# Block-sparse attention with a maxout MLP on one core: v spread by engine copies instead of DMA, maxima of k by a tree, masks and w2-w1 on Pool

## The chip, the core and the metric

The kernel runs on one core of a Trainium2 chip. The engines are TensorE (PE in the profile; PEld is its weight load), VectorE (DVE), ScalarE (ACT), Pool (POOL, GpSimd) and SyncE (SP, which here issues the DMAs). The metric is the time of one execution on the device in microseconds. Every kernel was run several times, beside runs of the kernel before on the same chip. A run is called slow when it is over 1.5% above the fastest of the same kernel; ratios use fast runs alone. A ratio is the mean time of one kernel's fast runs over that of the other's fast runs of the same rounds, so it is not quite the ratio of the medians that are quoted.

## The reference, cut to what matters

```python
# q, k, v: 4 batches, 8 heads, 768 positions, 64 wide
k_sum = k.reshape(B, H, 24, 32, D).max(axis=3)      # one key per block of 32: the maximum
v_sum = v.reshape(B, H, 24, 32, D).mean(axis=3)     # one value per block: the mean
scores_l = scale * q @ k.T, kept where |i - j| < 16 # a band
scores_s = scale * q @ k_sum.T + log(32)            # all 24 blocks
a = softmax over both; attn = a @ [v, v_sum]
x = attn as 3072 x 512
out = maximum(x @ w1, x @ w2) @ w_out               # d_ff 1024
```

The kernels compute the last line as x·(w1·w_out) + relu(x·(w2-w1))·w_out, so that w2-w1 is made once. TensorE does the same matmul work before and after the change (only the block means of v of the first batch come in two halves). (PSUM below is where the kernels place the tiles called `banks`, which their matmuls write; SBUF is where they place all other tiles.)

## The kernel before

Queries go in tiles of 64. A tile's keys are 64 positions on partitions 0 to 63, the 24 block sums on 64 to 95, and 32 positions on 96 to 127. Odd tiles need other partitions of v than even ones, so v has to move across partitions. After the first batch this is done by five DMAs per batch, and a sixth spreads the block means:

```python
for piece, (lo, hi, tiles_, part, ms) in enumerate((
        (0, 64, slice(0, NT, 2), 0, slice(0, NM)),
        (0, 64, slice(1, NT, 2), 64, slice(0, NM)),
        (96, 128, slice(0, NT, 2), 64, slice(0, NM)),
        (96, 128, slice(1, NT - 1, 2), 0, slice(1, NM)),
        (96, 128, slice(NT - 1, NT), 0, slice(0, 1)))):
    # vx[b][lo:hi, tiles_] <- vb[part:part + hi - lo, ms], by DMA
# ... means by TensorE, one copy on VectorE, one DMA "vx<-vx" to the other tiles
```

Per pair of heads, VectorE prepares k with four instructions (`prep`), and it masks the exponentials of the second to fourth batch:

```python
op("DVE", 0.96, ... tensor_copy(out=kt()[:, :, 0:64], in_=order(kps)))        # place k, from PSUM
op("DVE", 0.95, ... tensor_reduce(out=ks, in_=kt() by blocks of 32, op=max))   # 768 -> 24
op("DVE", 0.17, ... tensor_copy(out=kx[:, 96 * NT:KW], in_=kx[:, 0:32]))       # wrap
op("DVE", 0.22, ... tensor_copy(out=kt()[:, :, 64:88], in_=ks repeated))       # sums to all tiles
# scores on TensorE, exp on ScalarE, then
op(mask_on, ..., tensor_tensor(out=pv(), in0=pv(), in1=mask, op=mult))         # mask_on = "DVE"
```

The order of instructions on each engine is fixed when the kernel is built. A small scheduler in the kernel (`Plan`) takes the microseconds that stand in each `op(...)` and a lag per engine ("SP": 2.0 from a load's end to its use), and issues everything in that order. At run time an engine whose next input is late waits, even if inputs of later work are there: in the profiled run before, TensorE stood for 1.75 us, until 70.42, before values products that needed v's spread (L460), while inputs of matmuls ordered behind them were written (`g` of L581 by 64.97; they began at 70.89).

The softmax here doesn't subtract the row's maximum and nothing guards it: scores larger than these inputs give would overflow.

## Time and profile before

Median 193.4 us (192.1 to 195.2). First the page's line of busy times and, from its second part, three rows of 40 slices of 4.8 us (busy tenths) and the clock granted to TensorE:

```profile
PE 166.4 (86%) x1643; PEld 117.9 (61%) x1664; DVE 109.9 (57%) x289; ACT 114.1 (59%) x173; POOL 25.7 (13%) x39
...
PE   0629619899999969999979999999999999999990
DVE  6908956888979438759868953079777600000000
PEclk9999996999999999999999999999999999999999
```

From the ninth slice on (38 us) TensorE shows 9 everywhere but in two slices and the last; most of the holes are before that. The groups of VectorE instructions that the change touches (line, engine, operation, output and inputs, shapes, count | busy us in all, mean ns of one | idle before):

```profile
L375 DVE TENSOR_REDUCE ks<-kx 128x24 bf16<-128x768 bf16 x16 | 15.1, 944 | 0.1
...
L435 DVE TENSOR_TENSOR pb<-pb,mask 128x512 bf16<-128x512 bf16 x24 | 11.0, 464 | 3.1 <-ACT pb L426 3.1
...
L441 DVE TENSOR_TENSOR pb<-pb,mask 128x256 bf16<-128x256 bf16 x24 | 7.9, 369 | 1.7 <-ACT pb L426 1.7
...
L506 DVE TENSOR_TENSOR wd<-wf,wf 128x1024 bf16<-128x1024 f32 x4 | 4.9, 1222 | 0.8 <-DMA wf<-in_moe_w_dram 0.8
...
L382 DVE COPY kx<-ks 128x288 bf16<-128x288 bf16 x16 | 3.7, 229 | 0.0
L379 DVE COPY kx<-kx 128x32 bf16<-128x32 bf16 x16 | 3.4, 215 | 0.0
```

Masks take 18.9 us of VectorE and w2-w1 takes 4.9; the preparation of a pair of heads (placing 955, then 944, 215 and 229 ns) takes 2.34 us.

Four pieces of the chain that ended last (start us, us, what) show what the change is after:

```profile
14.21 8.25 DMA vx<-vb
...
63.29 7.09 DMA vx<-vx
...
70.42 0.63 PE banks L460 x15
...
82.35 10.64 DMA vx<-vb
```

The chain runs three times through DMAs that spread v (first, second and third batch), and at 70.4 us TensorE's values products (L460) start again when the second batch's spread has landed.

Last, busy time by stage (window, its length, then each engine's busy us with its instruction count, granted clock, DMA share, GB/s). The first window is the first batch with the weights, the next two are the rest of the attention mixed with the MLP:

```profile
0.00:46.00 46.00, 29.32 (x322) 22.43 (x324) 33.03 (x85) 24.87 (x33) 16.30 (x31) 0.96 1.04 296
46.00:101.00 55.00, 51.12 (x532) 36.05 (x540) 41.22 (x102) 38.15 (x59) 6.26 (x6) 1.00 1.09 269
101.00:165.00 64.00, 63.13 (x660) 45.93 (x666) 35.67 (x104) 41.93 (x67) 3.17 (x2) 1.00 0.43 113
```

**An account of lost time.** A busy TensorE is not a fast one here (166.4 us busy, where 159.1 would do by the rates that follow), so one more reading is used throughout. In the chain, back-to-back matmuls take 0.056 us (128x128), 0.030 (128x65), 0.109 (128x256) and 0.216 (128x512). With these rates all matmuls of either kernel need 159.1 us. The loss up to a matmul is its end less the work ordered in front of it; time that TensorE spends at half its clock (3.4 us in the first batch of this run) counts as loss too. For the profiled run before, 24.1 us are lost until the last values product of the first batch, 2.7 more until that of the second, 2.1 until that of the third, none after, and 4.5 us are the tail of the last copy and store.

### The profile page before, as it was taken

To read this page: it belongs to the slowest core of one execution; us is meant where nothing else is said; L and a number is where in the kernel's file an instruction comes from. 1 tells how busy PE (TensorE), PEld (TensorE's weight loads), DVE (VectorE), ACT (ScalarE), POOL (GpSimd) and SP (SyncE) were. 2 spreads that over 40 slices of the span, in tenths; PEclk is the share of its full clock that TensorE was granted. 3 is DMA by queue.
4 is the path that set the end of the run, shared out by engine and by line. 5 is a ranking of instruction groups with operands and counts; after the bars stand their busy time and mean duration, and the time that the engine had idled before them with its cause. 6 is when DMAs were issued, how large, how long until landed. Compare 5 with 4: busy or idle time off the path is not lost.

```text
span 192.5 us, 4148 instructions
## 1 busy us (share of the span) xinstructions
PE 166.4 (86%) x1643; PEld 117.9 (61%) x1664; DVE 109.9 (57%) x289; ACT 114.1 (59%) x173; POOL 25.7 (13%) x39
## 2 busy tenths in 40 slices
PE   0629619899999969999979999999999999999990
PEld 0426419865757738758657767487696676665740
DVE  6908956888979438759868953079777600000000
ACT  2533964384689949219967955179986443342621
POOL 7556221300330003300003300000000000000000
PEclk9999996999999999999999999999999999999999
DMA  5999999999999999999999996061020111120303
GB/s 187 226 305 356 234 240 347 371 381 281 210 359 251 292 268 217 339 309 217 229 288 223 340 218 193 3 164 24 3 109 5 54 58 59 50 109 0 112 0 109
DMA packets 47859, 37.27 MB, mean 194 GB/s; under 512 B 26208, under 2 KB 43744, under 8 KB 47840
## 3 DMA queue, kind: packets, MB, share of 16 engines
q1 hardware_dynamic: 47840, 37.01, 71.8%
q8 instruction: 13, 0.21, 0.5%
q14 instruction: 6, 0.05, 0.1%
HBM read 25.17 MB, written 6.29 MB: 163 GB/s over the span
## 4 chain that ended last, share of the span: by engine, by line
PE 53%; DMA 33%; SPq 5%; DVE 4%; POOL 2%; issue 1%; ACT 0%; ACTq 0%
PE banks L581 17%; PE banks L560 16%; DMA vf<-in_v_dram 13%; DMA vx<-vb 10%; PE banks L574 7%; PE banks L460 5%; DMA wf<-in_moe_w_out_dram 4%; SPq L503 4%; DMA vx<-vx 4%; PE banks L414 3%; DMA kqf<-in_k_dram 2%; PE banks L359 2%; POOL vb L340 2%; PE banks L484 2%; PE banks L313 1%; DVE pb L435 1%
## 5 line engine op out<-in xcount | busy, mean ns | idle before, releaser
L560 PE MATMUL banks<-xt,wd 128*128 128x256 bf16 x384 | 46.6, 273 | 0.5 <-DVE xt L489 0.5
L581 PE MATMUL banks<-wo,g 128*128 128x512 bf16 x184 | 44.9, 379 | 0.4
L560 PEld LDWEIGHTS <-wd 128*128 128x128 bf16 x384 | 36.4, 98 | 6.1 <-issue 0.7
L426 ACT ACTIVATE pb<-banks,bias 128x512 bf16<-128x512 f32 x48 | 31.5, 686 | 10.2 <-PE banks L414 9.9
L565 ACT ACTIVATE g<-banks 128x512 bf16<-128x512 f32 x48 | 28.3, 596 | 13.7 <-PE banks L560 13.2
L340 ACT COPY o<-banks 128x512 f32<-128x512 f32 x24 | 14.0, 585 | 28.7 <-PE banks L581 28.4
L388 ACT COPY qx<-banks 64x768 bf16<-64x768 bf16 x32 | 25.3, 791 | 6.1 <-PE banks L359 5.8
L581 PEld LDWEIGHTS <-g 128*128 128x128 bf16 x192 | 17.2, 97 | 16.5
L460 PE MATMUL banks<-vx,pb 128*128 128x65 bf16 x384 | 19.4, 196 | 3.6 <-DMA vx<-vx 1.8
L574 PE MATMUL banks<-w1o,xt 128*128 128x512 bf16 x85 | 21.9, 379 | 0.6
L460 PEld LDWEIGHTS <-pb 128*128 128x128 bf16 x384 | 16.9, 100 | 7.1 <-DMA vx<-vx 2.1
L359 PE MATMUL banks<-identity,kqb 128*128 128x128 bf16 x192 | 16.6, 234 | 5.3 <-DVE kqb L340 4.7
L340 ACT CAST kqb<-kqf 128x768 bf16<-128x768 f32 x16 | 13.1, 830 | 13.6 <-DMA kqf<-in_q_dram 8.7
L414 PE MATMUL banks<-qx,kx 128*128 128x128 bf16 (+2 forms) x208 | 18.6, 226 | 2.3 <-ACT qx L388 1.3
L340 POOL CAST vb<-vf 128x1536 bf16<-128x1536 f32 x8 | 12.2, 1520 | 55.0 <-DMA vf<-in_v_dram 35.2
L474 DVE TENSOR_TENSOR xs<-banks,inv 128x256 bf16<-128x256 f32 x48 | 19.1, 415 | 0.3
L414 PEld LDWEIGHTS <-kx 128*128 128x128 bf16 x208 | 15.1, 103 | 6.6 <-DVE kx L382 2.4
L359 PEld LDWEIGHTS <-kqb 128*128 128x128 bf16 x192 | 13.6, 106 | 8.5 <-DVE kqb L340 4.7
L373 DVE COPY kx<-banks 128x768 bf16<-128x768 bf16 x16 | 15.2, 955 | 2.9 <-PE banks L359 1.7
L375 DVE TENSOR_REDUCE ks<-kx 128x24 bf16<-128x768 bf16 x16 | 15.1, 944 | 0.1
L489 DVE COPY xt<-banks 128x512 bf16<-128x512 bf16 x24 | 9.8, 418 | 7.2 <-PE banks L484 6.8
L574 PEld LDWEIGHTS <-xt 128*128 128x128 bf16 x96 | 8.9, 98 | 7.9
(47 smaller groups left out, 129.8 us busy)
## 6 DMA issues: line engine op xcount, KB each, us to landing
kqf<-in_k_dram SPq DMA_DIRECT2D x16, 384.0 KB, 6.6
kqf<-in_q_dram SPq DMA_DIRECT2D x16, 384.0 KB, 5.7
vf<-in_v_dram SPq DMA_DIRECT2D x8, 768.0 KB, 10.7
out_dram<-o SPq DMA_DIRECT2D x20, 256.0 KB, 2.2
wf<-in_moe_w_dram SPq DMA_DIRECT2D x8, 512.0 KB, 11.1
vx<-vb SPq DMA_DIRECT2D x6, 396.0 KB, 8.0
wf<-in_moe_w_out_dram SPq DMA_DIRECT2D x4, 512.0 KB, 8.6
vx<-vx SPq DMA_DIRECT2D x4, 363.0 KB, 6.2
```

The lines of the kernel that those rows point to most:

```text
L340: {"DVE": nc.vector.tensor_copy, "ACT": nc.scalar.copy, "POOL": nc.gpsimd.tensor_copy}[engine](out=o, in_=i)
L359: nc.tensor.transpose(out=bank(ps, S, BF16)[:, 128 * j:128 * j + 128], in_=src.ap[:, j].rearrange("p h d -> p (h d)"), identity=identity[:])
L373: op("DVE", 0.96, lambda: nc.vector.tensor_copy(out=kt()[:, :, 0:64], in_=order(kps)), read=[kps], write=[kx[b, hp], kmain], prio=prio, la ...
L388: op("ACT", 0.8, lambda a=a, r=r: nc.scalar.copy(out=qx[b, hp].ap[r, a, :], in_=order(qps)[r]), read=[qps], write=[qx[b, hp]], prio=prio, ...
L414: nc.tensor.matmul(out=o[:, :, n0:n1], lhsT=w, rhs=qx[b, hp].ap[:, :, c:c + n1 - n0], start=(mask_on != "PE"), stop=(mask_on != "PE" or (i ...
L426: op("ACT", 0.7, lambda: nc.scalar.activation(out=pv(), in_=bank(ps).rearrange("p (i w q) -> p i w q", w=2, q=64), func=ACT.Exp, bias=bias ...
L460: nc.tensor.matmul(out=av()[:, u, a, :], lhsT=pb.ap[:, 2 * u + a, 64 * par:64 * par + 128], rhs=vx[b].ap[:, 4 * grp + 2 * u + par, 2 * hp ...
L474: op("DVE", 0.42, lambda: nc.vector.tensor_tensor(out=x.ap[:, hp % 2], in0=av()[:, :, :, 0:D], in1=inv.ap[:].to_broadcast([128, 2, 2, D]), ...
L560: nc.tensor.matmul(out=bank(ps)[:, 256 * s:256 * s + 256], lhsT=wd[n].ap[:, c, 128 * s:128 * s + 128], rhs=x.ap[:, c, :], start=(c == 0), ...
L565: op("ACT", 0.6, lambda n=n, ps=ps: nc.scalar.activation(out=g.ap[:, 2 * n:2 * n + 2, :].rearrange("p f n -> p (f n)"), in_=bank(ps), func ...
L574: nc.tensor.matmul(out=bank(ps), lhsT=x.ap[:, c, sl], rhs=w1o[c].ap[:], start=(c == 0), stop=False)
L581: nc.tensor.matmul(out=bank(ps), lhsT=g.ap[:, f, sl], rhs=wo[f // 2].ap[:, f % 2, :], start=False, stop=(f == FC - 1))
```

## The change

The intent is to get the spread of v off the DMA queues. Even tiles keep their order of keys and odd tiles get another one, so that most of v is already on the right partitions, and the rest moves by VectorE copies within its engine. To make room on VectorE, the maxima are taken by halving (a tree), and the masks and w2-w1 go to Pool. The core of the diff:

```diff
-        op("DVE", 0.95, lambda: nc.vector.tensor_reduce(... 768 -> 24 ...))
-        op("DVE", 0.17, ... wrap k)
-        op("DVE", 0.22, ... sums k, all 12 tiles)
+        op("DVE", 0.28, lambda: ... tensor_tensor(out=fold(16), in0=e[:, :, 0:16], in1=e[:, :, 16:32], op=ALU.max))
+        op("DVE", 0.18, lambda: ... tensor_tensor(... 16 -> 8, op=ALU.max))
+        op("DVE", 0.27, lambda: nc.vector.tensor_reduce(... 192 -> 24 ...))
+        for us, at, n, to, frm in ((0.2, 64, 64, ...), (0.14, 0, 32, ...), (0.1, 0, 32, ...)):
+            op("DVE", us, ... tensor_copy(out=kx[:, 1, to, at:at + n], in_=kx[:, 0, frm, at:at + n]))   # odd k
+        for e, at in ((0, 96), (1, 32)):
+            op("DVE", 0.2, ... sums k, 6 tiles each)
...
-            pbs[hp, grp] = scores(b, hp, grp, p + 5 + grp, "DVE")
+            pbs[hp, grp] = scores(b, hp, grp, p + 5 + grp, "POOL")          # masks, batches 2 to 4
...
-        load_w12(n, (30, 50, 150, 170)[n], 400)
+        load_w12(n, (30, 50, 150, 170)[n], 400, "POOL", "ACT")              # w2-w1, w1 cast
...
-        # v: two casts, five DMA pieces, one DMA of the means
+        # v: cast straight into the even tiles; per batch three copies to the odd tiles,
+        # two copies of the sums from PSUM, two copies that repeat them in five more key tiles, all on VectorE
```

Also w1 is cast on ScalarE instead of Pool, six zeroings go to ScalarE, and v of the first batch is loaded and handled in two halves and cast on VectorE. The exponential loses its bias (the factor 32 of the block sums is now carried by v's extra column), v has one load buffer for eight heads instead of two for four each, and w1's transposes get a buffer of their own.

## The prediction

> **What bounds the kernel now.** TensorE. The page has it busy 166.4 of 192.5 us; in the chain of waits, back to back, 8 matmuls of 128x512 take 1.73 us and 8 of 128x256 take 0.87 us, and with such rates all its matmuls need about 159 us (my sum). The other 33 us are a slow start, holes and a 4.5 us tail. The first values product runs at 29.8 us, behind the v spread by DMA (landed 29.0; the windows show TensorE busy only 14.2 of the first 30 us). By 43.4 us about 20 us of matmul work are done. From there to the last matmul (188 us) only some 6 us are lost, 1.75 of them at 68.5 us on the second batch's spread. DMA is saturated to about 125 us, but after 35 us TensorE fills in with maxout work, so most of that is hidden.
>
> **Removed, added, moved.**
> - DMA: all spreads (5.5 MB; near 27 us of the 16 engines' time). Loads come earlier: w_out starts landing near 35 us instead of 38.9, v of the second batch is complete near 48 instead of 54.1.
> - VectorE per batch: masks go (11.0+7.9 us over three batches, 6.3 each); w2-w1 goes once (4.9). Added: v copies, sums and their spread, about 5 us (from 64x3168 in 0.98 us alone, 32x512 in 0.69). Key preparation stays level: the 0.94 us reduction becomes about 0.75, the 0.4 us wrap and sums 0.85.
> - Pool: 36 masks at an estimated 1.1 us, w2-w1 4 x 2.1, v casts in one piece of 3 us. Busy rises from 26 to about 70 us.
> - ScalarE: zeroing and w1 casts (4 x 1.05), early.
> - TensorE work stays.
>
> **On the critical path.** The v chain of the first batch becomes VectorE work in order: summed from 4.1 us on, I reach the first values at about 28 us, with 1.8 us more matmul work done than before. VectorE then paces that batch to 42 to 44 us. Gain 2 to 3 us. The second batch's values can stall: v landed 48, cast 51, then VectorE copies behind key work, ready about 60 to 62, while TensorE's order wants them near 58. Later batches have over 10 us of slack.
>
> [...] mask products under a Pool cast took 1.22, 1.40 and 1.64 us instead of 0.28 and 0.41; a 0.16 us copy took 1.03. About half of the Pool cast time became VectorE waiting; with some 16 us of Pool reads per batch I expect 6 to 8 us more VectorE time per batch, giving back 4 to 7 us in TensorE stalls. [...]
>
> **Prediction.** 189.8 us, 8 in 10 between 184 and 196. Faster by over 2%: 0.42; within 2%: 0.47; slower by over 2%: 0.11.
>
> **Right or wrong shows in:** first values product near 28 us; no DMA in the chain after 40 us; TensorE gaps after 43 us released by VectorE or Pool, 4 to 7 us; short VectorE copies taking 0.5 to 1.5 us under Pool masks; matmul work unchanged.
>
> **What would make it wrong.** [...] Pool masks so late that values stall each batch (then above 196)[...].

One term of the sum: 184 us, for the case that VectorE hardly waits for Pool. With the 4 to 7 us of stalls on top the sum is 188 to 191 us. The masks' 1.1 us and the 2.1 us of w2-w1 on Pool were no measurements but the durations that the changed kernel gives its scheduler; 3 us for a cast of v is twice the 1.52 us that the half-size casts took before. For "saturated to about 125 us" the trace has a DMA share of 1.04 to 1.14 in every 10 us from 10 to 110 us, 0.91 to 120 us and 0.30 to 130 us.

## The result, and the profile after

The changed kernel takes 201.6 us (201.4 to 201.9, four runs) against 193.4 us: ratio 1.044, 95% interval 1.039 to 1.049. It is slower by 4.4%; 189.8 us with a range to 196 had been predicted. The page's busy times and slices (5.0 us each):

```profile
PE 171.1 (86%) x1670; PEld 120.3 (60%) x1670; DVE 130.3 (65%) x338; ACT 116.5 (58%) x183; POOL 76.8 (38%) x89
...
PE   0579554999996998999978699998899999999991
DVE  6579999886799889759999964059979251000000
PEclk9999996699999999999999999999999999999999
```

VectorE did not get lighter; it went from 109.9 to 130.3 us. After 50 us TensorE had two slices below 9 (a 6 and a 7) in the kernel before; now it has seven (two 6s, a 7 and four 8s), the last slice left out. The groups that answer to those of before:

```profile
L446 POOL TENSOR_TENSOR pb<-pb,mask 128x512 bf16<-128x512 bf16 x24 | 30.8, 1299 | 55.5 <-ACT pb L437 55.2
...
L452 POOL TENSOR_TENSOR pb<-pb,mask 128x256 bf16<-128x256 bf16 x24 | 17.7, 758 | 0.2 <-ACT pb L437 0.2
...
L393 DVE COPY kx<-ks 128x192 bf16<-128x192 bf16 x32 | 11.6, 405 | 0.1
...
L324 DVE COPY vx<-vx 32x2560 bf16<-32x2560 bf16 x6 | 8.9, 1479 | 0.2
...
L374 DVE TENSOR_TENSOR half<-kx 128x384 bf16<-128x384 bf16 x16 | 7.2, 449 | 0.2
...
L382 DVE TENSOR_REDUCE ks<-half 128x24 bf16<-128x192 bf16 x16 | 5.4, 340 | 0.0
L389 DVE COPY kx<-kx 128x384 bf16<-128x384 bf16 x16 | 5.1, 316 | 0.0
L378 DVE TENSOR_TENSOR half<-half 128x192 bf16<-128x192 bf16 x16 | 5.0, 315 | 0.0
L389 DVE COPY kx<-kx 128x160 bf16<-128x160 bf16 x16 | 4.4, 274 | 0.0
```

A pair of heads now costs VectorE 0.95 for placing, 0.45 + 0.32 + 0.34 for the tree, 0.32 + 0.27 + 0.19 for odd k and 2 x 0.41 for the sums, together 3.65 us instead of 2.34. Times 16 pairs that is 21 us, as much as VectorE's whole rise. The masks, w2-w1 and the rest that left it were eaten by the v copies.

A mean of 405 ns hides two kinds of instruction: half of the 32 took 202 ns or less, one took 2811. This is the stretch of the timeline where that one stands (start, us, engine, line):

```profile
74.77 1.29 POOL L452 TENSOR_TENSOR pb<-pb,mask 128x256 bf16<-128x256 bf16 x2
75.02 1.08 DVE L389 COPY kx<-kx 128x160 bf16<-128x160 bf16 x2
76.01 2.75 POOL L334 CAST vx<-vf 128x3072 bf16<-128x3072 f32 x1
76.01 2.81 DVE L393 COPY kx<-ks 128x192 bf16<-128x192 bf16 x1
```

The copy, which takes 0.20 us at the median, ends 0.06 us after Pool's cast, begun at the same moment: by these times it waited for the whole of it. The profile counts all 2.81 us as busy time of VectorE, not as waiting. A second one, at 98.39 us, took 1.16 us and ended 0.07 us after a mask product that Pool had begun 0.28 us before it. By the trace of this run three kinds of VectorE instruction can stretch beside Pool instructions that read: copies between SBUF tiles (up to 2.81 us), casts between them (that of k 1.28 us, 0.55 at the median) and products of two SBUF tiles (384 wide 1.21 us, 0.35 at the median). They are called exposed below. Reductions do not stretch (192 to 24: 0.32 to 0.34 us the four times that a reading Pool instruction ran beside them, 0.32 to 0.35 otherwise), nor does placing k from PSUM (0.94 to 0.96 us, both beside one, seven times, and without).

Busy time by stage, in the windows of before:

```profile
46.00:101.00 55.00, 51.47 (x495) 33.49 (x491) 46.46 (x104) 32.56 (x53) 27.99 (x21) 1.00 0.73 211
101.00:165.00 64.00, 58.84 (x658) 42.94 (x655) 44.95 (x124) 39.36 (x65) 28.18 (x31) 1.00 0.18 61
```

The DMA share falls from 0.43 to 0.18 in the last window, as intended, but VectorE rises by 5 and 9 us and Pool by 22 and 25. In the chain there is no DMA of v any more after the first batch; instead it runs through VectorE for 20 us on end (88.8 to 109.5 us, in the third batch) before TensorE comes next in it, with the transposes of the MLP's input (L495). An excerpt:

```profile
91.66 1.49 DVE vx L324
93.17 1.49 DVE vx L324
94.68 0.36 DVE half L374
...
98.39 0.71 DVE kx L393
...
100.16 1.14 DVE vx L334
...
109.48 0.29 PE banks L495 x2
```

And TensorE waits for VectorE (what waited, for whom, us in total, times, longest). The same two waits in the kernel before, then in the changed one:

```profile
PE banks L414 <- DVE kx L382: 1.0, 1, 1.0
PE banks L460 <- DMA vx<-vx: 1.8, 1, 1.8
...
PE banks L425 <- DVE kx L393: 4.3, 5, 1.6
PE banks L471 <- DVE vx L324: 3.5, 4, 1.5
```

L425 (before L414) are the scores, which need the k sums; L471 (before L460) are the values. In the account of lost time: 25.2 us until the end of the first batch's values (before 24.1), then 4.0, 5.2 and 2.0 for the other three batches (before 2.7, 2.1 and 0), tail 4.2 (4.5). So 6.4 of the 7.2 us between the two profiled runs (199.7 against 192.5) lie after the first batch.

### The profile page after: what moved, and what is told of

The parts are those of the page before. It is cut to its first block, busy times and chain, and to the rows that moved or that the text cites. A ratio compares the mean times of both kernels' runs of the same rounds, so it can differ in the third digit from the quotient of the medians.

```text
span 199.7 us, 4301 instructions
## 1 busy us (share of the span) xinstructions
PE 171.1 (86%) x1670; PEld 120.3 (60%) x1670; DVE 130.3 (65%) x338; ACT 116.5 (58%) x183; POOL 76.8 (38%) x89
## 4 chain that ended last, share of the span: by engine, by line
PE 52%; DVE 21%; issue 4%; POOL 3%; ACT 1%; DVEq 0%; ACTq 0%
PE banks L571 15%; PE banks L592 15%; PE banks L585 7%; DVE vx L324 4%; PE banks L471 4%; PE banks L555 3%; DVE kx L368 3%; PE banks L425 2%; DVE kx L393 2%; POOL pb L446 2%; DVE vx L334 2%; PE banks L495 2%; DVE vx L318 2%; PE banks L312 1%; DVE xs L485 1%
## 5 line engine op out<-in xcount | busy, mean ns | idle before, releaser
L446 POOL TENSOR_TENSOR pb<-pb,mask 128x512 bf16<-128x512 bf16 x24 | 30.8, 1299 | 55.5 <-ACT pb L437 55.2
L592 PE MATMUL banks<-wo,g 128*128 128x512 bf16 x192 | 46.5, 379 | 0.0
L437 ACT ACTIVATE pb<-banks 128x512 bf16<-128x512 f32 x48 | 27.2, 597 | 17.4 <-PE banks L425 15.2
L334 ACT COPY o<-banks 128x512 f32<-128x512 f32 x24 | 14.0, 585 | 32.5 <-PE banks L592 32.3
L399 ACT COPY qx<-banks 64x768 bf16<-64x768 bf16 x32 | 25.3, 791 | 4.8 <-PE banks L353 4.5
L471 PE MATMUL banks<-vx,pb 128*128 128x65 bf16 x384 | 20.6, 197 | 4.8 <-DVE vx L324 3.5
L425 PE MATMUL banks<-qx,kx 128*128 128x128 bf16 (+2 forms) x208 | 18.7, 224 | 6.5 <-DVE kx L393 4.3
L353 PE MATMUL banks<-identity,kqb 128*128 128x128 bf16 x192 | 17.7, 242 | 6.9 <-DVE kqb L334 4.8
L585 PE MATMUL banks<-w1o,xt 128*128 128x512 bf16 x96 | 23.2, 379 | 0.0
L471 PEld LDWEIGHTS <-pb 128*128 128x128 bf16 x384 | 17.7, 100 | 8.9 <-issue 4.8
L425 PEld LDWEIGHTS <-kx 128*128 128x128 bf16 x208 | 15.0, 102 | 11.4 <-DVE kx L393 7.2
L452 POOL TENSOR_TENSOR pb<-pb,mask 128x256 bf16<-128x256 bf16 x24 | 17.7, 758 | 0.2 <-ACT pb L437 0.2
L334 DVE COPY vx<-vx 64x3072 bf16<-64x3072 bf16 (+5 forms) x15 | 15.0, 1017 | 0.3
L483 DVE RECIPROCAL inv<-banks 128x4 f32<-128x4 f32 x48 | 8.0, 173 | 10.2 <-PE banks L471 10.1
```

The costliest lines, as they stand in the source:

```text
L334: {"DVE": nc.vector.tensor_copy, "ACT": nc.scalar.copy, "POOL": nc.gpsimd.tensor_copy}[engine](out=o, in_=i)
L353: nc.tensor.transpose(out=bank(ps, S, BF16)[:, 128 * j:128 * j + 128], in_=src.ap[:, j].rearrange("p h d -> p (h d)"), identity=identity[:])
L399: op("ACT", 0.8, lambda a=a, r=r: nc.scalar.copy(out=qx[b, hp].ap[r, a, :], in_=order(qps)[r]), read=[qps], write=[qx[b, hp]], prio=prio, ...
L425: nc.tensor.matmul(out=o[:, :, n0:n1], lhsT=w, rhs=qx[b, hp].ap[:, :, c:c + n1 - n0], start=(mask_on != "PE"), stop=(mask_on != "PE" or (i ...
L437: op("ACT", 0.6, lambda: nc.scalar.activation(out=pv(), in_=bank(ps).rearrange("p (i w q) -> p i w q", w=2, q=64), func=ACT.Exp, scale=scale),
L446: eng.tensor_tensor(out=pv(), in0=pv(), in1=m, op=ALU.mult)
```

## Experiments

Three theories were put against each other. A: Pool's masks and w2-w1 make VectorE wait, and the change gives VectorE many short exposed instructions. B: VectorE simply has more work, and chains get longer, contention aside. C: the fixed order of instructions was made with too short durations.

In this table "lost" is the account above in us for the profiled run, up to the end of the first batch's values, then the sum over the other three batches; the ratio is to the kernel before in the same rounds. The profiled runs of b_masks_pool and b_wd_pool were slow ones, so their "lost" is not used. The last column is the time at half clock that the trace of the profiled run records in these two stretches; half of it is the most that it can have added to "lost" (an estimate from the distance of back-to-back matmuls: in the profiled run before 0.107 us at half clock instead of 0.056 for 128x128, 0.055 instead of 0.029 for 128x65).

| kernel | ratio (95% interval) | median us | lost in batch 1 | lost in batches 2-4 | half clock, us |
|---|---|---|---|---|---|
| before | 1 | 193.4 | 24.1 | 4.8 | 3.4 / 0 |
| changed kernel | 1.044 (1.039-1.049) | 201.6 | 25.2 | 11.2 | 6.8 / 0 |
| x_masks_fill | 1.007 (0.997-1.018) | 194.9 | 25.2 | 4.7 | 6.8 / 0 |
| x_wd_fill | 1.042 (1.030-1.054) | 201.4 | 25.3 | 11.1 | 13.7 / 0 |
| x_both_fill | 1.006 (0.992-1.020) | 194.1 | 23.9 | 4.4 | 10.2 / 0 |
| x_spread_small | 1.025 (1.012-1.037) | 197.7 | 25.8 | 6.7 | 6.8 / 0 |
| x_masks_dve | 1.008 (1.001-1.015) | 195.3 | 27.7 | 1.9 | 10.2 / 0 |
| x_one_reduce | 1.041 (1.031-1.051) | 202.3 | 27.6 | 9.8 | 13.7 / 0 |
| x_true_times | 1.024 (1.016-1.032) | 200.4 | 24.6 | 9.1 | 6.8 / 3.4 |
| v_masks_times_lag | 1.011 (1.005-1.017) | 197.4 | 30.4 | 2.6 | 17.1 / 0 |
| v_masks_wd_times_lag | 0.998 (0.994-1.002) | 194.5 | 25.5 | 3.4 | 6.8 / 0 |
| b_masks_pool | 0.988 (0.978-0.998) | 192.6 | | |  |
| b_masks_pool_2 | 1.002 (0.996-1.009) | 193.3 | 23.1 | 4.6 | 3.4 / 0 |
| b_wd_pool | 1.001 (0.992-1.010) | 194.3 | | |  |
| b_masks_pool_lag | 1.008 (1.004-1.013) | 196.8 | 25.1 | 6.4 | 6.8 / 0 |
| b_copies | 1.006 (0.997-1.015) | 195.5 | 25.3 | 3.9 | 3.4 / 0 |
| b_masks_pool_copies | 1.030 (1.021-1.038) | 199.9 | 23.7 | 11.3 | 3.4 / 6.8 |
| b_masks_pool_reduce | 1.007 (1.002-1.013) | 194.0 | 23.8 | 6.2 | 6.8 / 3.4 |

Medians are over all runs of a kernel, slow ones too, and the chips differ: the fast runs of the kernel before had means between 192.8 and 194.8 us. The ratios are the figures to compare. The changed kernel itself was timed in the first call only. In the four fills (x_masks_fill to x_spread_small) only two of seven runs of the kernel before count as fast (192.9 and 193.3; the others took 195.8 to 198.3), so those four ratios hang on two runs. Within the call no such run is needed: the fast runs of x_wd_fill, which behaves like the changed kernel, average 201.2 us, those of x_spread_small 197.8, of x_masks_fill 194.5 and of x_both_fill 194.2.

### x_masks_fill: Pool just as busy, but without reading

```diff
-                eng.tensor_tensor(out=pv(), in0=pv(), in1=m, op=ALU.mult)
+                for _ in range(2):
+                    eng.memset(pv(), 1.0)
```

The half-size masks get the same edit. The order on every engine is that of the changed kernel. Its output is wrong, which doesn't matter for the time.

> Wrong result on purpose. The changed kernel with the same order on every engine; each of the 36 mask products on Pool is replaced by memsets of the same tile that take about as long (1.0 to 1.2 us) but read nothing. Theory A [...]: the short VectorE copies under Pool masks go back to 0.2 to 0.35 us, VectorE busy falls from 130 to about 118 us, and the time falls by 3 to 5 us, from 201.6 to 197 to 198.5. Rival B (VectorE simply has more work and longer dependency chains, contention aside): less than 1 us.

```profile
PE 168.2 (87%) x1651; PEld 119.2 (62%) x1670; DVE 121.9 (63%) x338; ACT 116.4 (60%) x183; POOL 73.8 (38%) x137
...
L393 DVE COPY kx<-ks x32: 191/203/1304, 7.7 to 147.8; 128x192 bf16<-128x192 bf16 x32
```

(The second line is of the view of one tile: shortest, median and longest of the 32 sums copies in ns. In the changed kernel they are 173, 202 and 2811.) The ratio falls from 1.044 to 1.007, more than expected, and the loss in batches 2 to 4 falls from 11.2 to 4.7 us, with first-batch loss unchanged at 25.2. VectorE's busy time falls to 121.9 us without one instruction less, and the longest sums copy takes 1.3 instead of 2.8 us. As Pool is about as busy as before (73.8 against 76.8 us) and the clock is alike (0.979 and 0.981 in the profiled runs), it is the reading and not Pool's lateness that costs. Theory A holds for most of the time that was lost. The cut is not even complete: copies are still held up, though less, beside Pool instructions that only write (three that take 1.3 us took 3.00 beside them in the next experiment).

### x_wd_fill and x_both_fill: the same for w2-w1, and both

```diff
-            out=wd[n].ap[:], in0=fs[1].ap[:], in1=fs[0].ap[:], op=ALU.subtract)
+            # a product of 2 columns (keeps the wait for the loads), then
+            nc.gpsimd.memset(wd[n].ap[:], 0.01); nc.gpsimd.memset(wd[n].ap[:], 0.01)
+            nc.gpsimd.memset(wd[n].ap[:, 0:2], 0.01)
```

> Wrong result on purpose. The changed kernel in the same order; each w2-w1 on Pool becomes memsets of about 2.4 us behind a product of two columns (which keeps the wait for the load). Theory A: the odd copies of v of the first batch go from 1.9 and 2.7 us to about 0.55 each, the first values product starts near 27 us instead of 30.2, the time falls by 1 to 3 us. Rival B: under 0.5 us, as VectorE's own work sets that start.

> Wrong result on purpose. Both of the edits before: masks and w2-w1 on Pool read nothing, same order. Theory A: the sum of both, 5 to 7 us less, near 195 us; what then remains over the kernel before (193.4) is VectorE's extra work. Rival B: under 1.5 us.

Alone, the edit changes nothing (1.042): a miss for theory A as I had put it. But the test did not remove the contention. The three odd copies of v of the first batch's second half, which the changed kernel's timeline has at 4.77 us together, still took 3.00 us under the memsets; the first half's three took 1.3 us undisturbed. Besides, TensorE got half its clock from 22.3 to 29.1 and from 32.5 to 39.3 us in this profile, and in the changed kernel's only from 31.6 to 38.4. (The 30.2 us of the expectation is the start of the second half's values in the changed kernel; the first 16 values products start at 27.5.) Both edits together are no better than the masks alone (1.006 against 1.007). What w2-w1 on Pool costs is not settled by these two.

### x_spread_small: less VectorE work, Pool untouched

```diff
-                    out=rs(lo, lo + 32, slice(1, NM)),
+                    out=rs(lo, lo + 32, slice(1, NM))[:, :, :, 0:D if b < 2 else 2],      # and the input alike
```

Same order, wrong result. The two copies of 1.48 us per batch that repeat the block sums nearly vanish in the third and fourth batch.

> Wrong result on purpose. The changed kernel in the same order; in the third and fourth batch the spread of the block sums of v over the key tiles (two copies of 32x2560, 1.48 us each) copies 2 of 64 columns. Theory A: at most 0.7 us faster, since these copies are not slowed by Pool. Rival B (VectorE's added work itself stalls TensorE): 2 to 4 us faster, the gaps near 103 and 140 us shrink.

The ratio falls to 1.025, and the loss of the third batch from 5.2 to 2.7 us, of the fourth from 2.0 to 0.1. So theory B holds too: work alone, of instructions that Pool did not slow (in the changed kernel all six took 1.475 to 1.484 us, and no Pool instruction ran beside any of them), stood on the chain. These copies repeat their input; copies of the same 32x2560 that do not took 0.815 us at the shortest.

### x_masks_dve: masks back on VectorE

```diff
-                pbs[hp, grp] = scores(b, hp, grp, p + 5 + grp, "POOL")
+                pbs[hp, grp] = scores(b, hp, grp, p + 5 + grp, "DVE")
```

> The changed kernel with the masks back on VectorE (the scheduler orders anew); correct result. Theory A [...]: VectorE takes 17 to 19 us of masks back but waits 12 us less, the time falls to 195 to 198 us. Theory B (VectorE's amount of work): VectorE busy near 137 us and the time stays at 200 us or more. If both hold, between: 197 to 200.

Ratio 1.008, correct result. VectorE's busy time hardly moves (132.7 against 130.3 us), although the masks take 15.8 us there (18.9 in the kernel before, where some waited for Pool's casts, up to 1.64 us instead of 0.42). So the rest of VectorE's work takes 13.4 us less. The loss in batches 2 to 4 is 1.9 us, the smallest of all. VectorE does the masks itself in little more time than it lost to Pool's doing them.

### x_one_reduce: the tree undone

```diff
-        # 384-wide maximum, 192-wide maximum, reduction of 192
+        op("DVE", 0.28, lambda: nc.vector.tensor_reduce(out=ks.ap[:, 0:nb], in_=even() by blocks, op=ALU.max))
+        # the two other entries stay in the plan and issue nothing, so that the order stays
```

> The changed kernel in the same order with the two halving maxima and the short reduction made one reduction of 768 again (0.94 us, no second input). Correct result. If the tree saves nothing even undisturbed (its parts take 0.35 + 0.25 + 0.34 us when Pool is idle) and only adds two instructions that wait for Pool: 1 to 2 us faster than 201.6. If the tree is a gain: 1 to 2 us slower.

No difference that the timing can show (1.041 against 1.044, and 1.031 to 1.051 is 2 us to either side), so the expected 1 to 2 us were neither found nor excluded. In the account batches 2 to 4 lose 1.4 us less than in the changed kernel and the first 2.4 more, with twice the time at half clock there. What can be said is that no gain of the tree shows. Undisturbed its parts take 0.35 + 0.25 + 0.34 = 0.94 us, the single reduction takes 0.944. That fits a fixed part of each instruction of 0.14 to 0.15 us, an estimate from two sizes of a kind, if the rest goes with the size: products of 384 and 192 take 0.35 and 0.25 us, reductions of 768 and 192 take 0.944 and 0.34 (the shortest copies here, of 32 elements, took 0.158 at the median). Three instructions pay it three times.

### x_true_times: the order made with the durations of the trace

```diff
-        op("DVE", 0.28 ... 0.18 ... 0.27            # tree
+        op("DVE", 0.35 ... 0.25 ... 0.34
-        "POOL": (1.1, 1.2)                          # masks; odd copies, sums and w2-w1 likewise
+        "POOL": (1.2, 1.4)
```

> The changed kernel, its scheduler given the durations that the trace shows undisturbed (maxima 0.35, 0.25, 0.34 us instead of 0.28, 0.18, 0.27; odd copies 0.25, 0.20, 0.16 instead of 0.20, 0.14, 0.10; spread of the sums 1.48 instead of 0.75; masks on Pool 1.2 and 1.4 instead of 1.1 and 1.2; w2-w1 2.4 instead of 2.1). Rival C (the static order, made with too short durations, costs the time): 4 us or more faster, to 197.5 or less. Theories A and B (the waits and the work cost it whatever the order): at most 2 us faster.

Ratio 1.024, against 1.044: two points, which are 3.9 us of 193.4. That is more than the 2 us that A and B allowed and just short of theory C's 4 us; the interval (1.016 to 1.032) does not decide between them. In the profiled runs the loss falls by 2.7 us in all, although this one has 3.4 us more at half clock. Theory C has a share, as large as that of less spreading. The single effects add up to more than the whole: masks without reads (3.7 points), less spreading (2.0) and better times (2.0) against 4.4. My reading, which no run shows by itself, is that all three cure the same thing: VectorE being later than the order of TensorE assumes.

### b_masks_pool, b_wd_pool: one part of the change alone, on the kernel before

```diff
-                pbs[hp, grp] = scores(b, hp, grp, p + 5 + grp, "DVE")
+                pbs[hp, grp] = scores(b, hp, grp, p + 5 + grp, "POOL")
```

```diff
-        op("DVE", 1.2, lambda: nc.vector.tensor_tensor(out=wd[n].ap[:], ...
+        op("POOL", 2.35, lambda: nc.gpsimd.tensor_tensor(out=wd[n].ap[:], ...
```

> The kernel before with this part of the change alone: masks of the second to fourth batch on Pool. Theory A: VectorE gets rid of 19 us of work, [...] 1 to 5 us slower than before. Theory B: VectorE has less work, so no slower and up to 2 us faster.

> The kernel before with w2-w1 on Pool alone. VectorE is rid of 4.9 us between 25 and 39 us, where after 30 us it paces the first batch[...]. Expected 0.5 to 2 us faster; if the start is set by the spread by DMA alone, within 0.5 us.

Masks on Pool do no harm to the kernel before (0.988 from two fast runs, then 1.002 in the repeat below), which contradicts theory A as expected here (1 to 5 us slower). w2-w1 on Pool changes nothing (1.001). So the same move costs the changed kernel 3.6 points (1.044 against 1.008) and the kernel before nothing. The theory needs another part: what else is on VectorE.

### b_masks_pool_2, b_copies, b_masks_pool_copies, b_masks_pool_reduce: which VectorE work makes masks on Pool dear

To the kernel before, per pair of heads of the second to fourth batch, either five short copies of the shapes of the changed kernel's odd copies and sums are added, or one reduction. Both write a spare tile that nobody reads, and stand on the way to the scores in the scheduler.

```diff
+            op("DVE", us, lambda m=m, n=n: nc.vector.tensor_copy(
+                out=spare[:, 0:m, 0:n], in_=kt()[:, 0:m, 0:n]), read=[kmain], write=[kx[b, hp]], ...)
```

```diff
+        op("DVE", 0.95, lambda: nc.vector.tensor_reduce(
+            out=spare[:, 0, 0:24] ..., in_=kt()[:, :, 0:64] by blocks, axis=AX.X, op=ALU.max), ...)
```

> A repeat of b_masks_pool on the chip of the three that follow. Was 1.2 percent faster than before; expected 0 to 1.5 percent faster.

> The kernel before, masks on VectorE, with five short extra copies per pair of heads in the second to fourth batch (about 1.0 us undisturbed, of the shapes of the changed kernel's odd copies and sums; they write a spare tile, and the result stays right). Pool only casts v here. Exposure: at most 1 percent slower than before. Load: 1 to 2 percent slower, as VectorE gets 12 us more work without the masks leaving it.

> The same extra copies with the masks on Pool. VectorE's work without waits is 7 us below that of b_copies. Exposure: the 60 copies meet masks and stretch by 6 us or more in all; 1.5 to 3 percent slower than b_masks_pool_2 and slower than b_copies. Load: no slower than b_copies.

> Masks on Pool and, instead of the copies, one extra reduction of 768 (0.94 us, not stretched under Pool in any trace so far). Exposure: within 1 percent of b_masks_pool_2 and clearly faster than b_masks_pool_copies. Load: as slow as b_masks_pool_copies, within 0.5 percent.

The added copies with masks on VectorE (b_copies), from the groups by shape:

```profile
L270 DVE COPY spare<-kx 128x192 bf16<-128x192 bf16 x24 | 4.8, 202 | 0.5
L270 DVE COPY spare<-kx 128x384 bf16<-128x384 bf16 x12 | 3.0, 250 | 0.0
L270 DVE COPY spare<-kx 128x160 bf16<-128x160 bf16 x12 | 2.4, 202 | 0.2
L270 DVE COPY spare<-kx 128x32 bf16<-128x32 bf16 x12 | 2.0, 169 | 0.2
```

The same copies with masks on Pool (b_masks_pool_copies):

```profile
L270 DVE COPY spare<-kx 128x192 bf16<-128x192 bf16 x24 | 9.9, 412 | 0.7
L270 DVE COPY spare<-kx 128x160 bf16<-128x160 bf16 x12 | 6.2, 517 | 0.3
L270 DVE COPY spare<-kx 128x384 bf16<-128x384 bf16 x12 | 5.3, 440 | 0.0
L270 DVE COPY spare<-kx 128x32 bf16<-128x32 bf16 x12 | 3.8, 316 | 0.4
```

And the added reduction with masks on Pool (b_masks_pool_reduce):

```profile
L269 DVE TENSOR_REDUCE spare<-kx 128x24 bf16<-128x768 bf16 x12 | 11.3, 939 | 0.0
```

The same 60 copies take 12.2 us in one kernel and 25.2 in the other. The reduction keeps its 0.94 us. Accordingly the copies cost 2.8 points with masks on Pool (1.030 against 1.002) and 0.6 with masks on VectorE, and the reduction costs 0.5. VectorE is equally busy in b_copies and b_masks_pool_copies (119.2 and 119.0 us), yet 1.006 and 1.030 are far apart, so the sum of VectorE's time does not decide. Part of that distance is clock: the runs of b_masks_pool_copies took 197.1 and 197.9 us at a mean clock of 0.99 and 199.9 at 0.974, and of b_copies the two at 0.96 and 0.97 (196.4, 196.6) count as slow and are left out. At equal clock the two kernels are 1.7% apart, and b_masks_pool_copies is 2.6 to 3.1% behind b_masks_pool_2. This answers the question: masks on Pool and short copies on VectorE are cheap alone and dear together, a reduction is not, and the change adds masks on Pool and short copies at once. That it matters that the copies stand on the way to the scores is argued; no run moved them elsewhere.

### v_masks_times_lag, v_masks_wd_times_lag, b_masks_pool_lag: looking for a better version

```diff
-    LAG = {"PE": 0.25, "ACT": 0.2, "DVE": 0.15, "POOL": 0.2, "SP": 2.0}
+    LAG = {"PE": 0.25, "ACT": 0.2, "DVE": 0.15, "POOL": 0.2, "SP": 3.5}
+    # v_...: masks on VectorE and the durations of x_true_times; v_masks_wd_...: w2-w1 on VectorE too
```

> The changed kernel with masks on VectorE, the durations of x_true_times, and 3.5 instead of 2.0 us from a load's end to its use in the scheduler (the trace shows the first loads landing 1.5 to 2 us later than planned, and TensorE waiting 2 us in order for the first w1 cast). TensorE's loss from the end of the first batch's values on was 2 us with masks on VectorE against 5 before; if the first part loses no more than before's 24 us: 190 to 192, faster than the kernel before by 1 to 2 percent. If the first part stays at 26 to 28 us: 193 to 196.

> As v_masks_times_lag with w2-w1 on VectorE too: nothing that reads runs on Pool while the first batch's v is copied. If the odd copies' waits under w2-w1 (4.8 us for three copies that take 1.3 undisturbed) set the first part, 1 to 2 us faster than v_masks_times_lag; if VectorE's sum of work sets it, 1 to 3 us slower.

> The kernel before with masks on Pool and the same 3.5 us for loads in the scheduler. b_masks_pool was 1.2 percent faster than before with an interval that nearly touches zero; if that is real, this too is 0.5 to 2 percent faster than before; if it was chance, within 0.5 percent.

With masks and w2-w1 on VectorE, the longer durations and the later lag, the changed kernel equals the one before (0.998): in this arrangement spreading v by VectorE copies and by DMA come out the same. The pair of v kernels differ only in w2-w1 and the order that follows, and the one with w2-w1 on Pool is 1.3 points slower and loses 30.4 instead of 25.5 us in the first batch; but its profile also has half clock for 17.1 instead of 6.8 us there, which alone may make up to 5.1 us (an estimate: half of the difference), and the orders differ. So the share of w2-w1 stays open. The later lag made b_masks_pool no better (1.008). No version was faster than the kernel before by 2%.

## Why the prediction was wrong

VectorE's waiting for Pool was named, and what it would cost came out at the upper end: masks that read nothing give back 3.7 points, about 7 us, where 4 to 7 were predicted. **The step that failed is the gain that was set against it.** The record had 184 us for the case that VectorE hardly waits for Pool, 9 us below the kernel before; its text accounts for 2 to 3 of them, and after the first batch only 4.8 us were lost. The runs show no such gain: with masks that read nothing the ratio is 1.007, with w2-w1 that reads nothing as well 1.006, and the masks alone taken off VectorE in the kernel before give 0.988 and 1.002. The fills leave part of the waiting in, so how small the gain is stays open; but no run of any version was faster than 190.3 us. The terms:

- **"Key preparation stays level."** This term failed. Predicted were 0.75 and 0.85 us for the tree and for odd copies with sums; undisturbed they take 0.94 and 1.01 (medians of the groups; b_copies has 1.03 for such copies), and with the waits for Pool it was 1.10 and 1.59. With the placing that makes 3.65 instead of 2.34 us per pair. I had taken the scheduler's guesses for 384- and 192-wide instructions (0.28, 0.18 and 0.27 us for the tree, where the trace has 0.35, 0.25 and 0.34 undisturbed). At these sizes the fixed part, estimated above at 0.14 to 0.15 us, is a large share of each.
- **"6 to 8 us more VectorE time per batch, giving back 4 to 7 us in TensorE stalls."** The second figure held, partly by luck. The first would be 18 to 24 us over the three batches with masks on Pool; x_masks_dve frees 13.4. So there was less waiting, and more of it reached TensorE. The waiting had been read from the few collisions before (five instructions took 4.6 us more than the medians of their groups, under six casts of v of 9.2 us in all: the "about half"). It was not counted that the change has 8 exposed instructions per pair of heads (the cast of k, two products, five copies) where before had 3 besides the masks, most of them in a row before the scores. Masks on Pool alone cost 3.6 points in the changed kernel and none in the kernel before. The loss after the first batch became 11.2 us, instead of 4.8.
- **"Later batches have over 10 us of slack."** The third batch lost 5.2 us. The slack was counted for v alone, but v's copies (1.48 us twice) sit in order on VectorE in front of the k work that the scores need. x_spread_small took this loss to 2.7 us. All work on v that was put at about 5 us per batch takes 6.4 undisturbed (sum of the shortest of each group).
- **"Gain 2 to 3 us" in the first batch.** The first values product did come at 27.5 us (28 predicted), but the loss until the batch's last values was 25.2 us, not 21 to 22. VectorE paced it to 46 us instead of 42 to 44. The three odd copies took 4.77 us under w2-w1 instead of 1.3, and TensorE had half its clock for 6.8 us (before 3.4; the difference may cost up to 1.7 us, an estimate). Half-clock stretches of 3.4, 6.8 and 10.2 us came in profiles of kernels with the same order, at differing times. How much of the first batch is clock and how much is w2-w1 stays open.

What was right: DMA left the chain after 40 us; v of the second batch landed at 47.8 us (48 predicted) and its values ran freely from 63.3 us (60 to 62); Pool's busy time reached 76.8 us (about 70); the matmul work is unchanged; short copies did stretch under Pool, even to 2.81 us.

## What to carry to other kernels

Before work is moved to Pool, count the VectorE instructions of the kinds that were exposed here (copies and casts between SBUF tiles, and products of two SBUF tiles: up to 2.81, 1.28 and 1.21 us instead of 0.20, 0.55 and 0.35) and see which stand in a row on the way to something TensorE wants; reductions and instructions that read PSUM were safe here (reductions of 192 took 0.32 to 0.35 us in the changed kernel, placing k from PSUM 0.94 to 0.96, whatever Pool did). A short instruction cost a fixed part here (an estimated 0.14 to 0.15 us, see x_one_reduce) and, when it was exposed, up to the rest of what Pool was doing (2.81 us beside a cast of 2.75), so splitting one 0.94 us instruction into three of the same sum gives more places to lose (0.94 became 1.10 us here). A mean that lies far above the shortest of a group (405 against 173 ns for the sums copies) is the sign of it in a profile, since such waits were counted as busy time (60 copies: 25.2 us instead of 12.2). And before a gain is set against a cost, ask how much time is there to win: here it was 4.8 us.
